# A state-space channel loop in a fixed, software-pipelined engine order, with phases and decay exponents from K=3 matmuls

## The chip, the cores and the metric

The kernel runs on one core of one Trainium2 chip. The time is the device time of one execution in microseconds (us), as the hardware profiler records it on that core. Engines are named as the profile names them: PE is TensorE (matmul), PEld its weight load, DVE is VectorE, ACT is ScalarE, POOL is GpSimd, and SP is SyncE, whose instruction stream issues the DMA transfers here ("SPq" in a timeline).

## The reference

The kernel computes a forward value and all gradients of a gated sum of two branches. One branch is softmax attention with 32 heads, the other a diagonal state-space convolution with 576 channels and 128 states per channel. Only the second branch matters here:

```python
def _B_ref(u, A_re, A_im, B_re, B_im, C_re, C_im, log_dt, Dskip):   # D = 576, N = 128, L = 2048
    dt = jnp.exp(log_dt)[:, None]
    logdA = dt * (A_re + 1j * A_im)
    P = jnp.exp(logdA[:, :, None] * l[None, None, :])      # decaying, rotating exponentials
    K = jnp.einsum("dn,dnl,dn->dl", Cc, P, dB).real        # one convolution kernel per channel
    ...                                                    # y = causal convolution of u with K
    return y + u * Dskip

g = sigmoid((x * gate_w).sum(-1))
out = g * attention(x) + (1 - g) * _B_ref(x, ...)
# returned: out and the gradients for the twelve inputs
```

## The kernel before

After the attention stage, which takes more than half of the time and which the change does not touch, the kernel goes through the 576 channels in blocks of 32. In each block it builds `E1e`, the exponentials for 128 time steps and 128 states, as exp(l·a) times (cos, sin)(l·θ). The products l·a and l·θ come from rows of a and θ that a DMA broadcasts over all partitions, and the phase is brought into range on DVE with the "add and subtract a large number" rounding:

```python
def egen(dG):                                   # 16 channels, called twice a block
    nc.sync.dma_start(abuf, <row of a, broadcast to 128 partitions>)      # 1 MB each
    nc.sync.dma_start(thb,  <row of theta, broadcast to 128 partitions>)
    nc.scalar.activation(abuf, abuf, ACT.Exp, scale=l0col)
    nc.vector.tensor_scalar(uk, thb, l0col, MAGIC, op0=A.mult, op1=A.add)
    nc.vector.tensor_scalar(uk, uk, -MAGIC, None, op0=A.add)
    nc.vector.scalar_tensor_tensor(thb, thb, l0col, uk, op0=A.mult, op1=A.subtract)
    ... Sin, Square, Sin on ScalarE; two products on VectorE give E1e
```

E1e goes through matmuls into `UV`. A serial scan of 14 steps over 15 chunks turns UV into states `HG`. GpSimd multiplies HG into the right side `Rw` of the output matmuls:

```python
for k in range(1, NS):                          # NS = 15, the serial scan
    nc.vector.tensor_tensor(tz, HG[:, :, k-1, :]..., ZZ, op=A.mult)
    nc.vector.tensor_tensor(t1v, t1v, UVk[:, :, :, k, :], op=A.add)
    nc.vector.tensor_tensor(HG[:, 0:2, k, :], tz[:, 0, 0:2], tz[:, 1, 2:4], op=A.add)
    nc.vector.tensor_tensor(HG[:, 2:4, k, :], tz[:, 0, 2:4], tz[:, 1, 0:2], op=A.add)
...                                             # casts of HG on ScalarE
for s in range(2):                              # rows of Rw, mostly on GpSimd
    for ri in range(2):
        nc.gpsimd.tensor_tensor(wa[:, ri], hv[:, ri], par[:, 8, :]..., op=A.mult)
        nc.gpsimd.tensor_tensor(wb[:, ri], hv[:, ri], par[:, 9, :]..., op=A.mult)
    nc.gpsimd.tensor_tensor(Rw[:, 0, ...], wb[:, 1], wa[:, 0], op=A.subtract)
    nc.vector.scalar_tensor_tensor(Rw[:, 1, ...], wa[:, 1], -1.0, wb[:, 0], ...)
...                                             # ybp matmuls, pairs, sums; closing sums on GpSimd
```

Further parts are `t0_stage` (loads Toeplitz windows `T0w` of the kernel row `Kp_d` just written to DRAM, and adds the matmul result `tps` to `ydi`, giving `yd`) and the mask path: `m_load` and `m_part` write `Md_d` to DRAM, and `m_sum` reads it back skewed (`skw`) for the matmul `dkp`. In this kernel a scheduler chooses the order of the instructions on every engine.

## Time and profile before

| | before |
|---|---|
| time, median of the runs beside the changed kernel | 4522.95 us (4520.06 to 4527.11, 4 runs) |
| profiled span | 4520.1 us |
| the loop, first scan to last scan | 3011.6 to 4310.7 us |
| one block of 32 channels | 76.4 us |
| DVE busy in one block | 51.6 us |

Part 1 of the page gives busy time, share of the span and number of instructions of each engine:

```profile
PE 3174.4 (70%) x24274; PEld 1144.6 (25%) x24274; DVE 2998.5 (66%) x5286; ACT 2869.0 (63%) x5049; POOL 475.8 (11%) x746
```

These are averages over stages with different limits, so they do not say what the change is worth. That is read inside the loop: how long a block is, how much of it the busiest engine works, and for what it waits in the rest. The prediction shows those views.

### The profile page before, as it was taken

What the parts mean: (1) busy time and instruction counts of PE and PEld (TensorE: products, weight loads), DVE (VectorE), ACT (ScalarE), POOL (GpSimd) and SP (SyncE); (2) the same over time, 40 slices, a digit from 0 to 9 for tenths busy, and PEclk for the clock granted to TensorE, in tenths of its full rate; (3) what the DMA queues carried; (4) which work ended last, traced back from release to release, by engine and by line L of the source; (5) the groups of instructions that cost most, each with busy time, mean ns of one, the idle gap of its engine ahead of it and who ended that gap; (6) DMA issues with size and microseconds to landing.
All of it is one profiled execution on the core that took longest, in us unless ns stands there. A gap on an engine that the chain in (4) does not pass through costs nothing. (4 is left out here: it accounts for less than half of the span.)

```text
span 4520.1 us, 64796 instructions
## 1 busy us (share of the span) xinstructions
PE 3174.4 (70%) x24274; PEld 1144.6 (25%) x24274; DVE 2998.5 (66%) x5286; ACT 2869.0 (63%) x5049; POOL 475.8 (11%) x746
## 2 busy tenths in 40 slices
PE   8889999999999999999999969523223232322211
PEld 2312222222222222222222215423222222212210
DVE  5437777677677776776777752247657657666668
ACT  5379989899899898998998931033334334333311
POOL 0000000000000000000000000003133233333420
PEclk9855555555555555555555559855555555555555
DMA  7346777767777667767667686656556554544437
GB/s 203 124 110 121 125 135 123 135 125 126 136 119 126 137 121 135 128 124 136 121 120 128 122 198 176 147 121 142 137 129 146 130 112 114 117 126 114 100 101 179
DMA packets 1755291, 595.14 MB, mean 132 GB/s; under 512 B 1666266, under 2 KB 1717404, under 8 KB 1745760
## 3 DMA queue, kind: packets, MB, share of 16 engines
q1 hardware_dynamic: 1754976, 590.99, 63.2%
q8 instruction: 191, 3.13, 0.3%
q14 instruction: 124, 1.02, 0.1%
HBM read 176.12 MB, written 60.67 MB: 52 GB/s over the span
## 5 line engine op out<-in xcount | busy, mean ns | idle before, releaser
L599 DVE TENSOR_TENSOR ds<-ps_P,PT 128x512 bf16<-128x512 f32 x2048 | 1329.1, 687 | 467.7 <-PE ps_P L30 261.5
L590 ACT ACTIVATE PT<-ps_P 128x512 bf16<-128x512 f32 x2048 | 1226.3, 603 | 139.0 <-PE ps_P L30 87.1
L594 ACT ACTIVATE eb<-ps_P 128x512 bf16<-128x512 f32 x2048 | 1236.0, 605 | 19.5 <-PE ps_P L30 19.0
L30 PE MATMUL ps_P<-dOaT,VaT_g 19*128 19x512 bf16 x2048 | 1197.2, 600 | 28.2 <-DMA VaT_g<-VaT_d 26.5
L30 PE MATMUL ps_P<-KaT_g,QaT_g 19*128 19x512 bf16 x2048 | 1164.0, 592 | 7.6 <-ACT PT L590 7.6
L30 PE MATMUL ps_P<-QaT_g,KaT_g 19*128 19x512 bf16 x2048 | 1053.6, 615 | 10.1 <-DMA KaT_g<-KaT_d 6.2
L30 PE MATMUL accO<-PT,Vtok_g 128*32 128x512 bf16 x2048 | 331.4, 632 | 0.0
L30 PE MATMUL accK<-dsT,Qtok_g 128*32 128x256 bf16 x4096 | 314.5, 407 | 2.0 <-DVE dqa L476 1.2
L30 PEld LDWEIGHTS <-KaT_g 19*128 19x128 bf16 x2048 | 135.6, 103 | 690.9 <-issue 665.1
L30 PEld LDWEIGHTS <-VaT_g 19*128 19x128 bf16 x2048 | 197.3, 98 | 434.4 <-issue 404.4
L30 PE MATMUL uvr<-RX,E1e 128*128 128x64 bf16 x576 | 99.9, 290 | 293.3 <-DVE E1e L842 292.5
L30 PE MATMUL accQ<-ds,Ktok_g 128*32 128x512 bf16 x2048 | 266.9, 620 | 1.2 <-DVE dvacc L459 1.2
L30 PE MATMUL accV<-eb,dOa 128*32 128x512 bf16 x2048 | 266.9, 621 | 0.6 <-DVE dkacc L500 0.6
L620 POOL MEMSET O_tok<- 128x1024 bf16 x1 | 1.0, 957 | 2429.3 <-DMA dqkv_d<-dtk 2429.3
L30 PE MATMUL ybp<-Rw,E1n 128*128 128x31 bf16 x1152 | 70.5, 233 | 234.5 <-POOL Rw L944 223.3
L30 PEld LDWEIGHTS <-E1e 128*128 128x128 bf16 x1152 | 120.0, 123 | 384.6 <-DVE E1e L842 301.4
L30 PEld LDWEIGHTS <-QaT_g 19*128 19x128 bf16 x2048 | 179.1, 100 | 51.3 <-issue 27.6
L476 DVE TENSOR_TENSOR dqa<-dqa,accQ 128x512 f32<-128x512 f32 x224 | 153.8, 687 | 49.0 <-PE accQ L30 48.7
L941 POOL TENSOR_TENSOR wa<-HG,par 128x480 f32<-128x480 f32 x72 | 99.8, 1386 | 772.8 <-DVE HG L924 769.7
L459 DVE TENSOR_TENSOR dvacc<-dvacc,accV 128x512 f32<-128x512 f32 x224 | 154.2, 688 | 37.1 <-PE accV L30 18.4
L30 PE MATMUL dkp<-sel,skw 128*128 128x8 f32 x144 | 37.9, 362 | 194.3 <-DMA skw<-Md_d 155.2
L834 ACT ACT_TABLE_LOAD x29 | 37.2, 1283 | 193.4 <-DMA abuf<-ath_d 193.0
(286 smaller groups left out, 4221.6 us busy)
## 6 DMA issues: line engine op xcount, KB each, us to landing
abuf<-ath_d SPq DMA_DIRECT2D x36, 1024.0 KB
thb<-ath_d SPq DMA_DIRECT2D x36, 1024.0 KB
T0w<-Kp_d SPq DMA_DIRECT2D x36, 512.0 KB
dsT<-ds SPq DMA_TRANSPOSE x512
dqkv_d<-dtk SPq DMA_DIRECT2D x96, 72.0 KB
dqkv_tok<-dqkv_d SPq DMA_DIRECT2D x1, 6912.0 KB
Md_d<-mst SPq DMA_DIRECT2D x144, 36.0 KB
ga_d<-ga_st SPq DMA_DIRECT2D x16, 288.0 KB
```

The source lines that it names most:

```text
L30: return nc.tensor.matmul(out, lhsT=lhsT, rhs=rhs, start=start, stop=stop, **kw)
L459: nc.vector.tensor_tensor(a_, a_, acc, op=A.add)
L476: nc.vector.tensor_tensor(U["dqa"], U["dqa"], acc, op=A.add)
L590: nc.scalar.activation(U["PT"][i][:, j, :], ps, ACT.Exp)
L594: nc.scalar.activation(e, ps, ACT.Exp)
L599: nc.vector.tensor_tensor(U["ds"][i][:, j, :], ps, U["PT"][i][:, j, :], op=A.mult)
L620: nc.gpsimd.memset(O_tok[:, :, D:DPAD], 0.0)
L834: nc.scalar.activation(abuf, abuf, ACT.Exp, scale=l0col)
L941: nc.gpsimd.tensor_tensor(wa[:, ri], hv[:, ri], par[:, 8, :].unsqueeze(1).to_broadcast([P, NS, CB]), op=A.mult)
```

## The change

The intent is to software-pipeline the loop by hand: while block i is scanned, block i+1's exponentials are built and block i+2's masks are prepared. The instruction order on PE, ACT, DVE and POOL is fixed to the order of the program. The scheduler still places the instructions of SP. Beside that:

- a and θ are split once into three bf16 terms that add up to them. The phases and exponents come out of K=3 matmuls into PSUM, in place of broadcast loads and DVE arithmetic.
- ACT does the rounding (Identity with the large number as bias), and DVE one subtraction per 512 columns.
- A scan step has three DVE operations in place of four.
- GpSimd's products move to DVE. The closing sums are kept for all channels in `SS` and done once at the end. Small copies move to ACT.
- Masks are handled per block of 32 channels, not per 64.

```diff
@@ setup
+                        for q in range(3):
+                            nc.vector.tensor_copy(spl[0:dsz, q, c, :], sc_[0:dsz, :])
+                            if q < 2:
+                                nc.vector.tensor_tensor(sc_, sc_, spl[0:dsz, q, c, :], op=A.subtract)
+                            nc.sync.dma_start(spl_d[r_, q, d0:d0 + dsz, :], spl[0:dsz, q, c, :])
@@ loop (cut; arguments shortened)
+                ctx.enter_context(tc.manual_schedule(engines={PE, Activation, DVE, Pool}))
+                def phase(b, h, q, which):
+                    ph = pps.tile([P, 4, N], F32, tag="ph", bufs=3)
+                    mm(ph, lhsT=lrow[r0:r0 + 3, :], rhs=B_["rw"][h][r0:r0 + 3, q * 4 * N:(q + 1) * 4 * N])
+                def ex(b, h):   # 4 x: Exp of a phase tile, 512 columns
+                def kk(b, h, q):
+                    nc.scalar.activation(kk[.., 4q:4q+4, :], ph, ACT.Identity, bias=magc, scale=1.0)
+                def ff(b, h, q):
+                    nc.vector.scalar_tensor_tensor(v_, v_, MAGIC, ph, op0=A.subtract, op1=A.subtract)
-                    nc.vector.tensor_tensor(HG[:, 0:2, k, :], ..., op=A.add)
-                    nc.vector.tensor_tensor(HG[:, 2:4, k, :], ..., op=A.add)
+                    nc.vector.tensor_tensor(HG[:, :, k, :], t0v, t1v[:, ::-1], op=A.add)
-                    nc.gpsimd.tensor_tensor(wa / wb ..., op=A.mult)
+                    nc.vector.tensor_tensor(B_[nm], HG, par[:, r_, :]..., op=A.mult)       # 1920 columns
+                        skw = pw.tile([P, P], F32, tag="skw", bufs=2)                      # was 3
+                        rr = pw.tile([P, 2, NS, CB], BF, tag="rr")                         # one buffer
+                for i in range(-1, NBLK + 1):            # the fixed order; nx: i+1 exists, mb = i + 2
+                    m_load(mb)
+                    kk(i+1, 0, 0); kk(i+1, 0, 1);  scan(i, 0, 4)
+                    ff(i+1, 0, 0); kk(i+1, 0, 2);  scan(i, 4, 7)
+                    ff(i+1, 0, 1); kk(i+1, 0, 3);  scan(i, 7, 10)
+                    ff(i+1, 0, 2); scan(i, 10, 12); ff(i+1, 0, 3); sn(i+1, 0)
+                    scan(i, 12, 15); casts(i)
+                    t0(i-1, 0); m_mask(mb); m_part(mb, 0); t0(i-1, 1); m_part(mb, 1)
+                    prod(i+1, 0); kk(i+1, 1, 0); kk(i+1, 1, 1); uv(i+1, 0); rw1(i)
+                    ff, kk of the second half;  rw2(i);  sn(i+1, 1)
+                    ybp(i, 0); ybp(i, 1); pairs(i); kp(i)
+                    prod(i+1, 1); uv(i+1, 1); sums(i)
+                    m_sum(mb); m_fin(mb)
+                    ex(i+2, 0); ex(i+2, 1)
@@ closing stage: 24 operations of 576 columns on DVE form the sums for all channels (cut)
```

## The prediction

> **What bounds the kernel now.** I read the whole-kernel page first, then busy time by stage, then the loop's vector instructions in time order, then the waits inside the loop. Part 2 of the page (forty slices) shows where the changed code lies:
>
> ```profile
> PE   8889999999999999999999969523223232322211
> DVE  5437777677677776776777752247657657666668
> POOL 0000000000000000000000000003133233333420
> ```
>
> PE is full up to slice 24; that is attention, which the change leaves alone. The state-space loop is the stretch from slice 27 to 38 in which POOL works and no engine is near full. Stage windows put numbers on it (columns: window, length, then busy us and instructions of PE, PEld, DVE, ACT, POOL, clock, DMA share, GB/s):
>
> ```profile
> 2895.00:3011.60 116.60, 26.93 (x216) 19.79 (x216) 34.09 (x48) 31.74 (x30) 0.24 (x1) 0.54 0.54 125
> 3011.60:4326.50 1314.90, 364.55 (x4801) 306.01 (x4802) 877.16 (x1643) 495.68 (x515) 434.66 (x663) 0.53 0.51 123
> 4386.00:4520.00 134.00, 20.38 (x136) 8.44 (x135) 111.90 (x226) 24.83 (x45) 0.00 (x0) 0.50 0.68 164
> ```
>
> Over 17 blocks, DVE has 877/17 = 51.6 us a block, ACT 29.2, POOL 25.6, PE 21.4. A block's length comes from the cast that opens each scan, in the timeline of DVE (start, duration, instruction, wait before it):
>
> ```profile
> 3011.63 0.23 DVE L917 CAST HG<-UV 128x128 f32<-128x128 bf16 x1 [3.55 <-ACT UV L904]
> ...
> 4172.02 0.23 DVE L917 CAST HG<-UV 128x128 f32<-128x128 bf16 x1 [3.55 <-ACT UV L904]
> 4236.33 0.23 DVE L917 CAST HG<-UV 128x128 f32<-128x128 bf16 x1 [3.35 <-ACT UV L904]
> 4310.68 0.23 DVE L917 CAST HG<-UV 128x128 f32<-128x128 bf16 x1 [3.92 <-ACT UV L904]
> ```
>
> (4310.68 - 3011.63)/17 = **76.4 us a block**. DVE is idle for 25 of them. The waits of DVE in the loop say on whom (total, times, longest):
>
> ```profile
> DVE Rw L945 <- POOL wa L941: 87.1, 32, 3.7
> DVE xs L791 <- DMA xs<-xs: 68.8, 24, 7.1
> DVE HG L917 <- ACT UV L904: 61.6, 12, 13.3
> DVE RX L740 <- DMA RX<-xr_d: 45.5, 5, 16.8
> DVE uk L835 <- DMA thb<-ath_d: 42.2, 16, 5.5
> DVE yd L861 <- ACT yd L860: 40.4, 14, 4.1
> ```
>
> So it is a loop of short waits with DVE as its busiest engine; the change can win DVE work and waits, and can add new waits because its order is fixed.
>
> [...]
>
> ```profile
> L972 DVE TENSOR_TENSOR pC<-UV,gR x36: 651/1645/1804, 3053.6 to 4334.0; 128x960 bf16<-128x960 bf16 x36
> L945 DVE SCALAR_TENSOR_TENSOR Rw<-wa,wb x36: 772/1634/1647, 3052.9 to 4337.9; 128x480 bf16<-128x480 f32 x36
> ```
>
> The pair product has a 1645 ns median beside POOL and 651 at best. [...] 2290 ns for 2048, 291 for 128. [...] The trace has 1283 ns, and loads only ahead of Exp and Sin. [...]
>
> **Part by part, per 32-channel block.** Successive independent DVE instructions start about 0.08 us sooner than their durations add up (1.63 us at 4200.64, the next at 4202.19); I subtract it.
>
> *Leaves DVE:* the phase arithmetic, 2 x (1.29 + 1.22 + 2.35) = 9.7 us, becomes 8 subtractions of 512 columns from PSUM at 0.61 (687 ns less overlap) = 4.9. The scan joins two HG adds (start to start 1.18 us a step, at 4236.59 and 4237.77) into one: 0.46 + 0.33 + 0.33 = 1.12, times 14 = 15.7. Pairs lose the POOL block: 3 x 1.08 + 2 x 0.54 + 1.08 + 6 x 0.32 = 7.3. Small copies go to ACT.
> *Comes to DVE:* POOL's products, 2 x 2.08 for 1920 columns; then 2 x 1.07 for the rows of Rw; together 6.3.
> *Stays:* products E1e 4 x 2.21 = 8.9, masks 2.5, yd 1.1, RX 0.9, first cast 0.2.
> Sum 4.9 + 15.7 + 7.3 + 6.3 + 8.9 + 2.5 + 1.1 + 0.9 + 0.2 = **47.8 us**, only some 4 below 51.6.
> *ACT:* 8 roundings at 0.6, 8 Exp at 0.51, 6 Sin and Square at 1.82, 8 UV at 0.5, 2 loads 2.6, the rest about 7: 33. [...] *DMA* loses 4 broadcasts of 1024 KB, but the queue was not the bound. POOL is empty.
>
> **The waits that the fixed order leaves,** walked with those durations from the moment when the last UV copy of a block lands (T):
> - *Exp before the next phases.* The last two skw loads stand behind a DMA transpose (4.8 to 5.1 us of queue time) in the SP order. That transpose waits for the last product at T-4.6, and the queue also does T0w then; so they land near T+5, the dkp sums reach ACT by T+6.8, then a table load 1.3, 8 Exp 4.1 and the first rounding 0.6: T+12.8. DVE has only 3 scan steps, done at T+3.6. **Wait 9.2.**
> - *One PSUM buffer for psM and tps.* After the last phase subtraction ACT does a load 1.3, three functions 5.5, casts 2.2 and the tps copy. Only then does psM start: 1.6 on PE, 0.6 on ACT, 1.1 for the second tps. From that subtraction this is 12.6, against 6.4 of DVE work (3 scan steps, yd, masks). **Wait 6.3.**
> - *One ybp buffer and one rr buffer.* Three functions 5.5, copies 0.7, second ybp 1.95, then two rounds of 30 sums (1.2) and rr (0.6), and a last rr: 12, against 7.3 of DVE work. **Wait 4.7.**
> - *UV after the last product:* 32 matmuls at 0.115 and the last copy, 4.6, partly under RX: **3.7.**
> Together 23.9, so 47.8 + 23.9 = 71.7, say 72. Table loads can run before their function is ready (one did at 2907.6, its Sin at 2928.4), which takes up to 1.3 off each of two waits; I count 1. **Block: 71 us**, minus 5.4.
>
> **Ends.** Prologue: half-size masks and no broadcast loads, first scan about 38 us sooner by the same walk. Drain: T0w has one buffer, plus 9. Closing sums for all channels: 24 DVE instructions of 576 columns at 0.67 = 16, in a stage where DVE is 112 of 134 us busy, so plus 16. The split into three: some 40 more small DVE operations in the first 170 us, under PE: plus 3. Together minus 10.
> Sum: 4521 - 17 x 5.4 - 10 = **4419 us**, I say 4420.
>
> **Rivals.** (A) *DVE becomes the bound and the waits vanish:* 48 us a block, 4521 - 17 x 28.4 - 10 = 4028. For it: the order was evidently written to fill DVE. Against: the four waits above are bound by single buffers and in-order ACT. (B) *The queue takes over:* every block now has mask loads, with 64-byte rows, and SP waits in order for Kp_d, transposes and skw; loads reached 21 us of wait before. At 78 us a block the time is 4521 + 27 - 10 = 4538, the same within 2%. For it: blocks with mask work took 80 to 86 us in places before, those after it about 71. Against: the broadcasts, the largest loads, are gone. (C) *Half the waits overlap:* 60 us a block, 4232.
>
> **Range and chances.** The sum is near the 2% line (4431); an error of 4 us a block is 68 us. I give more room to C than to B, since the change was made to shorten the loop. 4330 to 4490; faster 0.56, same 0.40, slower 0.04.
>
> **What would show it.** Right: scan-to-scan 69 to 73 us; DVE busy 46 to 49 of it; pair products at about 1.15 us for 1920; two table loads a block; DVE waits led by the first phase subtraction on ACT (7 to 9 us each), then yd on PE, rr on PE and HG on UV; first scan before 2980; attention unchanged. Wrong: a DVE wait near zero at the first subtraction (A or C), SP waits or skw above 10 us a block on the chain (B), or ex, Sin or K=3 matmuls of other durations than taken here.

The sum came to 4419 us, said as 4420. In the kernel before, the 2290 and 291 ns are of TENSOR_TENSOR instructions on DVE with f32 inputs, of 2048 and 128 columns, and the 1283 ns are of a table load on ACT. In the loop these loads stand only ahead of Exp and Sin; at 39.57 us one stands ahead of a Sqrt. The "POOL block" of the pairs is the same pC at 1.64 us while POOL worked (4271.02 us) and at 0.65 us when POOL was idle (4275.84 us). Two terms, 2.08 us for 1920 columns and 1.07 for 960, are estimates; a straight line through the 291 and 2290 ns gives 2.16 and 1.16 us for them, from which the overlap of 0.08 us goes off. The 0.67 for 576 columns is what TENSOR_TENSOR takes in the kernel before, 743 to 759 ns, less that overlap.

## The result

| | before | after |
|---|---|---|
| median of 4 runs | 4522.95 us | 4480.89 us (4480.74 to 4482.63) |
| ratio after/before | | 0.9907, 95% interval 0.989 to 0.9924 |
| profiled span | 4520.1 us | 4479.0 us |

A ratio is the mean time of one kernel's fast runs over the mean of the other's in the same rounds, so it is not quite the ratio of the medians quoted beside it. The change makes the kernel 0.9% faster. The forecast was 2.2%.

Parts 1 and 2 of the page of the kernel after, to be read against those of before:

```profile
PE 3291.8 (73%) x24562; PEld 1166.9 (26%) x24562; DVE 2927.3 (65%) x5146; ACT 2933.1 (65%) x5376; POOL 21.8 (0%) x45
```

```profile
PE   8889999999999999999999987833343333343411
DVE  5437777777677777776777771155656566565668
POOL 0000000000000000000000000000000000000000
```

POOL is empty, as intended, and DVE is more even over the loop, at five to six tenths. It is still not near full.

The stage window over 13 steady blocks of the kernel after (window, length, then busy us and instructions of PE, PEld, DVE, ACT, POOL, clock, DMA share, GB/s):

```profile
3107.60:4104.80 997.20, 375.44 (x3965) 257.44 (x3965) 599.69 (x1074) 431.48 (x638) 0.00 (x0) 0.52 0.39 74
```

That is 997.2/13 = 76.7 us a block, with DVE busy for 599.69/13 = 46.1 of them. The casts that open each scan, in the timeline of DVE of the kernel after:

```profile
2969.73 0.23 DVE L910 CAST HG<-UV 128x128 f32<-128x128 bf16 x1 [4.45 <-ACT UV L903]
...
3875.31 0.23 DVE L910 CAST HG<-UV 128x128 f32<-128x128 bf16 x1 [4.45 <-ACT UV L903]
...
4248.03 0.23 DVE L910 CAST HG<-UV 128x128 f32<-128x128 bf16 x1 [4.45 <-ACT UV L903]
```

(4248.03 - 2969.73)/17 = 75.2 us on average over all blocks, because the first block is shorter than the steady ones, with 61.2 us, and the last too, with 65.7. So the whole balance is: the loop 17 × (75.2 - 76.4) = -20 us; the first scan 3011.6 - 2969.7 = 41.9 us earlier; and the time from last scan to end longer by (4479.0 - 4248.0) - (4520.1 - 4310.7) = 21.6 us. Together -41 us, which is the difference of the spans. The loop, for which the change was written, gives only half of it.

What DVE waits for in those 13 blocks (total us, times, longest):

```profile
DVE kk L871 <- ACT kk L866: 183.9, 13, 16.1
DVE yd L1015 <- ACT yd L1013: 103.4, 26, 4.7
DVE rr L988 <- PE misc L30: 48.9, 26, 3.1
DVE HG L910 <- ACT UV L903: 46.5, 13, 4.5
```

Per block: 14.1 us at the first phase subtraction, 8.0 at yd, 3.8 at rr and 3.6 at UV, together 29.5. The waits of before (Rw on POOL, xs, RX and thb on DMA) are gone. These four have taken their place, and they are longer.

### The profile page after: what moved, and what is told of

The parts are those of the page before. It is cut to its first block, busy times and chain, and to the rows that moved or that the text cites. A ratio compares the mean times of both kernels' runs of the same rounds, so it can differ in the third digit from the quotient of the medians.

```text
span 4479.0 us, 64906 instructions
## 1 busy us (share of the span) xinstructions
PE 3291.8 (73%) x24562; PEld 1166.9 (26%) x24562; DVE 2927.3 (65%) x5146; ACT 2933.1 (65%) x5376; POOL 21.8 (0%) x45
## 5 line engine op out<-in xcount | busy, mean ns | idle before, releaser
L30 PE MATMUL psM<-xs,gyp 128*32 128x128 bf16 x576 | 42.3, 423 | 339.4 <-DVE xs L799 322.0
L871 DVE SCALAR_TENSOR_TENSOR kk<-kk,ph 128x512 f32<-128x512 f32 x144 | 95.1, 684 | 249.5 <-ACT kk L866 249.5
L30 PE MATMUL uvp<-RX,E1e 128*128 128x64 bf16 x1152 | 134.1, 290 | 111.9 <-DVE E1e L885 111.9
L30 PE MATMUL ph<-thr,lrow 3*128 3x512 bf16 x288 | 147.4, 591 | 64.0 <-DVE kk L871 20.7
L877 ACT ACTIVATE uk<-kk 128x2048 f32<-128x2048 f32 x36 | 68.8, 1911 | 176.0 <-DVE kk L871 175.9
L903 ACT ACTIVATE UV<-uvp 128x512 bf16<-128x512 f32 x144 | 86.0, 597 | 144.0 <-PE uvp L30 143.8
```

The source lines that it names most:

```text
L30: return nc.tensor.matmul(out, lhsT=lhsT, rhs=rhs, start=start, stop=stop, **kw)
L871: nc.vector.scalar_tensor_tensor(v_, v_, MAGIC, B_["ph"].pop((h, q)), op0=A.subtract, op1=A.subtract)
L877: nc.scalar.activation(uk, f_, ACT.Sin, scale=0.5 * TWO_PI * SIN_SAFE)
L903: nc.scalar.mul(UV[:, ri, :, c0:c0 + 8], pr, -1.0 if ri == 0 else 1.0)
```

## The experiments

Theory Q ("queue") was formed on the two traces. The first subtraction waits so long because the `skw` loads, which stand at the end of a pass, come late in SP's in-order stream. Two instructions, a T0w load and a transpose, stand between Kp_d's store and the skw loads. Timeline of SP in the kernel after (start, duration, instruction; T, the cast of this pass, is 3875.31):

```profile
3868.65 0.45 SPq L966 DMA_DIRECT2D Kp_d<-KT  x1
3874.60 0.39 SPq L1008 DMA_DIRECT2D T0w<-Kp_d  x1
3875.09 6.45 SPq L887 DMA_TRANSPOSE E1n<-E1e  x1
3881.64 1.38 SPq L825 DMA_DIRECT2D skw<-Md_d  x2
```

SP stands still for 5.5 us until Kp_d has landed, as T0w reads it; then it is held by the transpose for 6.45 us; only then, at T+6.3, do the last two skw loads go out. In the pass before, Kp_d's store is itself late. Its data are ready at 3788.96 us (the end of ACT's cast into KT), but the store leaves 4.4 us later, behind the xs copies in SP's stream (this view begins within them):

```profile
3784.26 9.03 SPq L794 DMA_DIRECT2D xs<-xs  x6
3793.39 0.45 SPq L966 DMA_DIRECT2D Kp_d<-KT  x1
```

ACT, in its fixed order, stands before the copies of the dkp sums. Timeline of ACT, same pass:

```profile
3885.42 0.19 ACT L832 CAST RX<-misc 128x32 bf16<-128x32 f32 x1 [9.93 <-PE misc L30]
...
3885.86 1.28 ACT L859 ACT_TABLE_LOAD   x1
3887.15 4.03 ACT L859 ACTIVATE ab<-ph 128x512 f32<-128x512 f32 x8
3890.99 1.91 ACT L866 ACTIVATE kk<-ph,magc 128x512 f32<-128x512 f32 x3
```

DVE's subtraction starts at 3891.78, T+16.5, and in the pass before (T = 3796.79) at 3816.36, T+19.6. The difference of the two passes, 3.1 us, is about that of the store's delay (4.4 us against 1.2). The rival was that the block is set elsewhere, so that taking this wait away only lengthens another. That the fixed order as such is the cost became a second rival when run 6 had shown it.

All runs gave correct outputs, with 4 runs each. The ratios are against the kernel before, whose medians were 4519.75 (first four experiments), 4524.5 (next four), 4516.45 (next four) and 4516.86 us (last three). The kernel after stands at 4480.89. Where two runs of different calls are compared below, some 8 us (the spread of these medians) are not clear of noise.

### 1. Four buffers for skw

```diff
-                        skw = pw.tile([P, P], F32, tag="skw", bufs=2, name="skw")
+                        skw = pw.tile([P, P], F32, tag="skw", bufs=4, name="skw")
```

> The changed kernel with four skw buffers in place of two, so that all four skw loads of a block stand ahead of Kp_d, T0w and the second transpose in the SP order; nothing else is moved. Queue theory: the 14.1 us a block that DVE waits at the first phase subtraction (184 us in 13 blocks of the changed kernel) come mainly from the last two skw loads, which land 10 to 13 us after the last UV copy. With them early, the four dkp matmuls end some 2 us after that copy, then table load 1.3, eight Exp 4.0, rounding 0.7: wait about 5 us a block, block 76.7 to 67 us, whole kernel 4481 to about 4325. Rival, ScalarE theory: the wait is the Exp and the table load themselves, which stand ahead of the rounding in any case: wait stays above 12 us a block, time above 4450.

Measured: 4334.11 us, ratio 0.9582 (0.9566 to 0.9598). The four loads now go out together, directly behind the transpose and ahead of the xs copies and Kp_d. Waits of DVE in this kernel, 3107 to 4000 us:

```profile
DVE kk L871 <- ACT kk L866: 66.0, 14, 4.9
```

The wait falls from 14.1 to about 5 us a block, and the time by 147 us, or 8.6 a block. Theory Q holds, and the expected time (about 4325) came out: the lack of two buffers of 64 KB cost 3% of the whole kernel.

### 2. The dkp sums and their copies later in ACT's order

```diff
                     if nx:
                         ff(i + 1, 0, 1); kk(i + 1, 0, 3)
+                    if 1 <= i + 1 < NBLK:
+                        m_sum(i + 1)
+                        m_fin(i + 1)
...
-                        m_sum(mb)
-                        m_fin(mb)
```

> The changed kernel with the dkp matmuls and their copies moved from the end of a pass to behind the fourth rounding of the next pass, two skw buffers as before. Queue theory: the chain is then last UV copy, table load 1.3, eight Exp 4.0, rounding 0.7, so the first subtraction waits 2 to 3 us in place of 14.1; block about 65.5 us, whole kernel about 4295, and 30 us under the run with four skw buffers. If the skw wait only moves with the dkp matmuls (PE in order ahead of the tps matmuls, which then come later), the wait at yd grows by several us and the time is 4330 to 4380. ScalarE theory: Exp still stands ahead of the rounding, so the time stays above 4450.

Measured: 4297.71 us, ratio 0.9507 (0.9493 to 0.9521). The order stays fixed, but ACT goes through the Exp and the first roundings before it waits for the sums:

```profile
DVE kk L871 <- ACT kk L866: 33.2, 13, 2.6
```

The wait is 2.6 us a block at most, and the expected time (about 4295) came out. Runs 1 and 2 shorten the same wait from two sides, by sending the loads earlier and by asking for them later. So the wait was on skw, passed on by ACT's order.

### 3. Toeplitz matmuls ahead of the scan's end

```diff
                     if cur:
                         scan(i, 7, 10)
+                    if i >= 1:
+                        t0(i - 1, 0)
...
+                    if i >= 1:
+                        t0(i - 1, 1)
                     if nx:
                         ff(i + 1, 0, 3)
...                                              # both removed from behind casts(i)
```

> The changed kernel with both tps steps moved up: the first behind scan step 9, the second ahead of the fourth phase subtraction, so that their ScalarE copies stand ahead of the Sin and Square and psM no longer takes turns with tps. Theory: the 8.0 us a block that DVE waits at yd (103 us in 13 blocks) come from that order; the wait falls below 1 us, block 76.7 to about 69 us, kernel about 4355. Rival: the first product E1e waits for Sin and Square in its place, some 6 us, and the time stays above 4440. A third outcome: the second T0w load is late at its new place, and the yd wait halves only.

Measured: 4355.1 us, ratio 0.9634 (0.9619 to 0.9648). The yd wait is gone, the first-subtraction wait stays at 14.3 us a block, and the block is about 8 us shorter. So this wait is worth about its own length, 17 × 8.0 = 136 us against 126 measured, and no other took its place.

### 4. Three buffers for rr

```diff
-                        rr = pw.tile([P, 2, NS, CB], BF, tag="rr", name="rr")
+                        rr = pw.tile([P, 2, NS, CB], BF, tag="rr", bufs=3, name="rr")
```

> The changed kernel with three rr buffers in place of one, so that DVE needn't wait for the PE sums (3.8 us a block). If the waits of a block simply add up, as the prediction added them: block 76.7 to 73 us, kernel about 4420. If the queue sets the time of the Exp (Kp_d landing, T0w, transpose, skw), DVE only arrives earlier at the first subtraction and waits longer there: the rr wait goes to 0, the wait at the first subtraction grows from 14.1 to about 17 us, and the time falls by less than 25 us, to 4455 to 4480.

Measured: 4391.98 us, ratio 0.9718 (0.9704 to 0.9733), so both expectations missed and the gain was larger than either. The rr wait is gone (3.8 us a block), and the first-subtraction wait fell by one more, to 13.1 us. The timeline of SP shows the second part: the scheduler, which still places SP's instructions, here put the transpose and the skw loads ahead of T0w, so that they no longer wait for Kp_d to land:

```profile
3814.26 0.45 SPq L966 DMA_DIRECT2D Kp_d<-KT  x1
3814.82 8.21 SPq L887 DMA_TRANSPOSE E1n<-E1e  x1
3823.14 1.38 SPq L825 DMA_DIRECT2D skw<-Md_d  x2
3824.61 0.41 SPq L1008 DMA_DIRECT2D T0w<-Kp_d  x1
```

The transpose takes longer there, so the stretch from Kp_d's store to the skw loads shrinks by less than the wait: from 12.2 to 13.0 us in the kernel after to 7.5 to 8.9 in every second block and 11.2 to 11.5 in the others. Why it chose another order is not shown. A buffer count on one engine thus changed another engine's order, and a one-line experiment was not a one-cause experiment.

### 5. The skw loads on GpSimd's queue

```diff
-                        nc.sync.dma_start(skw, src)
+                        nc.gpsimd.dma_start(skw, src)
```

> The changed kernel with one word changed: the skw loads are issued from GpSimd's own queue instead of the shared SP queue; two skw buffers, and every engine's order, as in the changed kernel. Queue theory: it is the place in the SP order that makes the last two skw loads late, so they land some 3 us after the first dkp matmuls; the wait at the first subtraction falls from 14.1 to about 7 us a block, block about 69 us, kernel 4345 to 4380, between the changed kernel (4481) and the run with four skw buffers (4334). Rival: two buffers are the cause (loads serialised by the dkp matmuls) or the loads themselves are slow: time stays above 4440.

Measured: 4427.4 us, ratio 0.9787 (0.9773 to 0.9802). The direction is right, and the size about half. With two buffers the third and fourth loads still wait for the matmuls of the first two (these start at 3547.37 us, the two loads go out at 3548.26), and a load took 4.2 us from issue to landing. In one pass the matmuls waited 5.16 us for these loads, and ACT's copies came some 7.8 us after the cast, in place of 10.1 and 13.2. So SP's order is one part of theory Q, and the two buffers, which put the loads one behind the other, are another.

### 6. No fixed order

```diff
-                ctx.enter_context(tc.manual_schedule(engines={PE, Activation, DVE, Pool}))
```

> The changed kernel without the fixed engine order: the line that takes the four engines from the scheduler is gone, everything else stays (matmul phases, GpSimd's products on VectorE, buffers, program order as priorities). It tells whether the small gain is due to the order or to the other parts. If the fixed order is what pays (its intent), the time rises to the kernel before or above, 4500 to 4600. If the order is what costs (waits of 30 us a block that a scheduler would fill), the time falls to 4250 to 4400. My own guess is the first, with some 4530, since single buffers leave a scheduler little room.

Measured: **4105.77 us**, ratio 0.9075 (0.9061 to 0.9088). My expectation was wrong by 400 us: I took the fixed order for the part that helps. One line removed is worth 375 us, nine times what the whole change won. The window 3107 to 3900 us of the kernel after, then of this one:

```profile
3107.00:3900.00 793.00, 297.77 (x3086) 201.89 (x3086) 471.49 (x856) 342.14 (x509) 0.00 (x0) 0.52 0.39 75
```

```profile
3107.00:3900.00 793.00, 402.70 (x4451) 280.07 (x4452) 662.05 (x1219) 544.06 (x757) 0.00 (x0) 0.56 0.58 102
```

In the same 793 us DVE works 662 us (83%) in place of 471 (59%). The block is (3829.73 - 2970.86)/16 = 53.7 us. The long waits have become many short ones:

```profile
DVE E1e L882 <- ACT kk L876: 27.5, 14, 2.5
DVE HG L908 <- ACT UV L901: 25.7, 14, 2.6
DVE yd L1013 <- ACT yd L1011: 23.9, 14, 2.0
DVE xs L797 <- DMA xs<-xs: 23.1, 17, 2.0
DVE kk L869 <- ACT kk L864: 15.2, 14, 1.3
```

The first subtraction waits about 1 us a block here. The scheduler puts masks, mask loads and rr where DVE would stand still, and spreads the Exp among ACT's other work. For that it pays with table loads: 103 of them over the loop in place of 35 (103 × 1283 ns = 132 us against 45 us of ACT), and the kernel is still 8% faster.

### 7. The Rw products back on GpSimd, order fixed

```diff
-                        nc.vector.tensor_tensor(B_[nm], B_["HG"]..., op=A.mult)
+                        nc.gpsimd.tensor_tensor(B_[nm], B_["HG"]..., op=A.mult)
```

> The changed kernel with one part undone: the two products of 1920 columns are back on GpSimd (one instruction each). If VectorE is relieved, its 4.2 us a block leave the chain and the time falls by up to 70 us. Contention and latency theory: on GpSimd the two take about 2 x 4.8 us (1.2 us for 480 columns in the kernel before), the two Rw instructions wait for them, since only 1.3 us of VectorE work stand between[...]: 4 to 8 us more a block, time 4520 to 4620.

Measured: 4484.36 us, ratio 0.9911 (0.9896 to 0.9926), the same as the kernel after. Neither number came out. The pair products of 1920 columns took 1150 ns, against 1158 in the kernel after. A product of 1920 columns takes 4250 ns on POOL against 2152 on DVE, which is 4.2 us less DVE work a block; but a mask product beside it took 3.83 us in place of 0.68, and the second half's subtraction waited 1.7 us. Together 3.15 + 1.7 us, which outweighs the 4.2: the steady block is 77.0 us in place of 76.7. So the run does not show that DVE's work is free in a loop that waits; the relief was lost again beside POOL.

### 8. All order mends at once, order fixed

rr and T0w get two buffers, both t0 come early as in run 3, the eight Exp stand behind the fourth rounding, and the dkp sums behind `sn(i+1, 0)`.

```diff
+                        ex(i + 1, 0); ex(i + 1, 1)            # behind kk(i + 1, 0, 3)
+                        t0(i - 1, 0)                          # as in run 3, likewise t0(i - 1, 1)
+                        m_sum(i + 1); m_fin(i + 1)            # behind sn(i + 1, 0)
+                        ... bufs=2 for rr and T0w; blk(i + 2) at the end of the pass
```

> All waits found taken away together: both tps steps early and two T0w buffers, two rr buffers, the eight Exp behind the fourth rounding (ScalarE is idle there while VectorE scans), the dkp sums behind the first Sin and Square. Expected from the changed kernel's trace: VectorE work 47.2 us a block plus 3.6 at UV plus 1 to 3 of new small waits, block 52 to 54 us, first scan about 2970 as before: kernel 4090 to 4130, faster than both. If the waits only change places (an engine or the queue takes over as bound), the block stays above 60 us and the time above 4220.

Measured: 4215.67 us, ratio 0.9316 (0.9301 to 0.9332), 86 us above the first expectation and just under the second (above 4220), with a steady block of 60.5 us. The first-subtraction wait is gone, but another has come:

```profile
DVE yd L1015 <- ACT yd L1013: 97.9, 13, 7.5
```

The Exp, which ran eight in 4.0 us, now start every 1.27 us, each after 0.67 us of waiting for its phase matmul; the tps copy stands behind them. The likely reason is that two of the three phase buffers hold rounded phases whose subtraction comes later, so that matmul and Exp alternate through one buffer. This is argued from the trace and was not tested.

### 9, 10, 13 and 14. Which engine's fixed order costs

The list of engines in the line of run 6 is cut down: ACT alone (9), DVE alone (10), PE alone (13), ACT and DVE (14).

```diff
-                ctx.enter_context(tc.manual_schedule(engines={PE, Activation, DVE, Pool}))
+                ctx.enter_context(tc.manual_schedule(engines={Activation}))      # 9; {DVE} in 10, {PE} in 13,
+                                                                                 # {Activation, DVE} in 14
```

> Fixed order kept on ScalarE alone; the scheduler orders TensorE, VectorE and GpSimd. The changed kernel has 4481 us, with no fixed order 4106. If ScalarE's order is what costs (Exp ahead of the next rounding, tps copies behind Sin and Square: two of the four waits of VectorE, 22 of 29.5 us a block, end on ScalarE in this order), most of the 375 us remain: 4300 to 4480. If VectorE's or TensorE's order costs, this run is near 4106 to 4200.

> Fixed order kept on VectorE alone. ScalarE theory: the scheduler can now put the dkp copies and Exp elsewhere, so the time is 4110 to 4220. Rival: VectorE's order costs, since it has nothing else to do in the program's order while it waits at the first subtraction and at yd: 4300 to 4480. If both this run and the one with ScalarE alone are near 4106, only the two orders together cost.

> Fixed order kept on TensorE alone. Without any fixed order 4106, with ScalarE's alone 4214 (+108), with VectorE's alone 4264 (+158), with all 4481 (+375). If the costs of the three orders add up, TensorE's alone costs the remaining 109: about 4215. If TensorE's order costs nothing by itself (its waits are short and its work is 28 us of a block): 4100 to 4140, and the rest of the 375 comes from two fixed orders meeting.

> Fixed order on ScalarE and VectorE, TensorE left to the scheduler, which can then put phase matmuls ahead of the dkp matmuls that wait for skw. If costs add: 4106 + 108 + 158 = 4372. If the fixed TensorE order is needed for the chain skw, dkp, Exp, the time is 4300 to 4400; if ScalarE's order holds the dkp copies ahead of Exp in any case (they stand in its program), the chain remains and the time is 4440 to 4490.

| order fixed on | median us | ratio (95% interval) | above run 6 |
|---|---|---|---|
| none (run 6) | 4105.77 | 0.9075 (0.9061 to 0.9088) | 0 |
| PE | 4160.43 | 0.9207 (0.9192 to 0.9223) | 55 |
| ACT | 4213.59 | 0.9329 (0.9315 to 0.9343) | 108 |
| DVE | 4263.74 | 0.944 (0.9426 to 0.9454) | 158 |
| ACT and DVE | 4476.17 | 0.9914 (0.9898 to 0.9931) | 370 |
| PE, ACT, DVE, POOL (the change) | 4480.89 | 0.9907 (0.989 to 0.9924) | 375 |

Runs 9, 10 and 13 fell between the ranges that had been expected for them; in run 14 the third, 4440 to 4490, came out. No single engine explains it: ACT and DVE alone add up to 266, and together they cost 370. The first-subtraction wait is one thing that appears only with both. DVE's waits, 3107 to 3900 us, with ACT alone fixed (run 9) and with ACT and DVE fixed (run 14):

```profile
DVE kk L871 <- ACT kk L866: 22.8, 26, 1.6
```

```profile
DVE kk L871 <- ACT kk L866: 157.4, 11, 16.6
```

That is 1.7 us a block in run 9 (here all its phase subtractions together) and 14.3, the full length, in run 14. With DVE alone fixed (run 10) this wait is not in the list at all, and the longest is another, for UV:

```profile
DVE HG L910 <- ACT UV L903: 124.5, 12, 12.9
```

So this wait arises only where the two fixed orders meet, while each order alone already costs 108 and 158 us by other waits. Fixing PE and POOL as well adds nothing clear of noise (ratios 0.9914 and 0.9907). The reading of the trace is that ACT may not pass the late dkp copies, and DVE may not do other work meanwhile.

### 11 and 12. What the parts are worth when the order is free

Both without the fixed order: in 11 the Rw products go back to GpSimd (the edit of run 7), in 12 the phase matmuls are undone.

```diff
-                        nc.scalar.activation(ab[:, 4 * q:4 * q + 4, :], phase(b, h, q, 1), ACT.Exp)   # run 12
+                    nc.sync.dma_start(ab, <row of a, broadcast to 128 partitions>)
+                    nc.scalar.activation(ab, ab, ACT.Exp, scale=l0col)
...                  # likewise theta: broadcast load and the three DVE operations of the kernel before
```

> Without the fixed order, and the two products of 1920 columns back on GpSimd. Here VectorE is the bound (779 of 940 us in the run without fixed order), so the placement matters. If relief counts, 4.2 us a block leave VectorE: down to 4040. If GpSimd's slowness (8 to 10 us for the two)[...] count, as in the kernel before, where the same-sized product took 1645 ns beside GpSimd against 651: VectorE loses more than it gains and waits for them, 4130 to 4250. I expect the second.

> Without the fixed order, and the matmul phases undone: decay and phase rows come as two broadcast loads of 1024 KB each for 16 channels, VectorE does the three phase operations as in the kernel before (9.7 us a block instead of 8 subtractions, 4.9), ScalarE does Exp in one instruction of 2048 columns. Work theory: VectorE is the bound, so the block grows by the 4.8 us, and by waits for the loads into one kk buffer (6 us each seen before): 53.7 to 59 to 65 us, kernel 4190 to 4300. If the matmul phases are worth little (their loads hidden, rounding through TensorE and ScalarE as long as on VectorE), the time stays within 4090 to 4150.

Measured: run 11 4192.3 us, ratio 0.9282 (0.9267 to 0.9298), 87 us above run 6, with DVE waiting for POOL's product 76.1/13 = 5.9 us each time; run 12 4267.52 us, ratio 0.9444 (0.943 to 0.9458), 162 us above run 6. Both expected ranges held. The second cause, from the expectation of run 11, is not shown: its pair products of 1920 columns took 1152 ns. The same move that cost nothing in run 7 costs 87 us here. The 162 us of run 12 are not DVE's own work alone: its longest wait there is for the mask loads, 87.4 us over 3107 to 3900 us against 23.1 in run 6:

```profile
DVE xs L799 <- DMA xs<-xs: 87.4, 45, 7.8
```

### 15. No fixed order, and the buffers of runs 1 and 4

The edits of runs 1, 4 and 6 together.

> No fixed order, and three rr and four skw buffers in place of one and two: a version meant to be faster than all so far. VectorE waits 7 to 8 us a block in the run without fixed order, little of it at rr (0.1 us) and none at skw, so the buffers can give at most 1 to 2 us a block: 4075 to 4110. If it is slower, the scheduler's order has changed for the worse.

Measured: **4077.71 us**, ratio 0.9027 (0.9013 to 0.904), the fastest of all and faster than both kernels. The buffers that are worth 147 and 89 us when the order is fixed are worth 28 together when it is free. The time lies at the lower end of the expected range.

## Why the prediction was wrong

The sum said 4420, the kernel took 4481. The balance of the 61 us: the average block was 75.2 us and not 71, 17 × 4.2 = 71 us too long; the ends won 10 us more than forecast.

**Right.** The prologue and drain: the first scan came 41.9 us earlier (38 forecast), the split cost nothing (attention began some 2 us earlier; plus 3 forecast), and the end took 21.6 us longer (9 + 16 forecast). DVE's work: 76.7 - 29.5 = 47.2 us of a block is not wait, against 47.8. Its parts hold too: pair products at 1158 ns for 1920 columns, and Rw products at 2152 ns. The K=3 matmuls start 0.44 us apart where three stand together (1.46 us for the three at 3885.32 us, 0.58 for one alone). There are two table loads a block, and the four waits are the four that were named, in that order of cost. Their causes hold in three cases: runs 1 and 2 for skw, run 3 for the place of tps, and run 4 for the single rr buffer.

**The step that failed first** is "they land near T+5, the dkp sums reach ACT by T+6.8 ... T+12.8. Wait 9.2". The loads were *issued* only at T+6.3 or later; the copies ran on ACT at T+10.1 in one pass and T+13.2 in the other; and the subtraction started at T+16.5 and T+19.6. The wait measured 14.1. I had counted the transpose and named T0w, but T0w entered as an issue of half a microsecond. It is a wait of SP on a DRAM write: 65.1 us in 12 times over the 13 blocks, 5.4 us each, in front of everything behind it. Two smaller parts of the same stream were mis-sized too: Kp_d's store left up to 4.4 us after its data were ready, behind the xs copies, and the transpose took 5.7 to 6.5 us, not 4.8 to 5.1. Runs 1 and 2 show that the late skw loads cause the wait; how the delay divides among the three parts was not tested, and run 4, which took the T0w wait away from ahead of the loads, gained only part of it. The mis-sized wait is 14.1 - 9.2 = 4.9 us of the 5.7 by which the steady block exceeds 71.

**The second mis-sized term** is yd: 8.0 us and not 6.3. The walk ended at "1.1 for the second tps" on PE. But DVE's add waits for ScalarE's copy of the same tps, and it waits twice, 4.7 us at the first tps and 3.2 at the second. It is an ACT wait, not the PE wait that I named. The rest is small: rr 3.8 and not 4.7, UV 3.6 and not 3.7, and the early table loads won the 1 us only in part. The load ahead of Sin ran while Sin waited (3818.42 against 3827.39 us); that ahead of Exp stood on the path. From the walk's 71.7: + 4.9 + 1.7 - 0.9 - 0.1 - 0.6 (work) = 76.7, the steady block.

**The rivals.** B ("the queue takes over") was right about the place, SP's in-order stream, and its 78 us a block was nearer than my 71. But it is no throughput limit, as the DMA share over 3011.6 to 4326.5 us fell from 0.51 to 0.38; it is the latency of one ordered chain, and two more small buffers undo most of it. A ("DVE becomes the bound and the waits vanish") was rejected on "the four waits are bound by single buffers and in-order ACT". Run 6 shows that only the second half was needed: with the same single buffers and a free order the block is 53.7 us, DVE is 83% busy, and the time is 4106, nearest to A's 4028. The argument for A, "the order was evidently written to fill DVE", was the wrong reason; the order is what keeps DVE from being filled. I gave the fixed order no cost of its own in any rival, and that is the larger mistake.

**Where the expected gain went.** The content of the change is worth 419 us (4524.5 to 4105.77 in run 6). Of it the phase matmuls carry 162 (run 12) and the products on DVE 87 (run 11), if the parts add up, which was not tested. The remaining 170 us (joined scan add, copies on ACT, deferred sums, smaller masks, pipelining by two blocks) were not separated. The fixed order gives 375 of them back.

**Open.** Why the scheduler changed SP's order in run 4, the phase-buffer reading of run 8, and how far a fixed order mended in all places could go: the best of mine with the order fixed was 4215.67 us, 138 above run 15.

## What to carry to other kernels

When a program's order is fixed on several engines at once, walk each in-order stream to its slowest foreign event, here a DRAM write of 8 KB that a later load on the DMA queue must see (5.4 us of wait on average), and ask who stands behind it. With the order fixed, one late load here became a wait of 7.5 us on PE, 9.9 on ACT and 12.9 on DVE in the same pass, so test the kernel with the order left free before crediting or blaming its parts. A part's worth depends on the order around it: moving the same products to GpSimd cost nothing in run 7 and 87 us in run 11.
